# Two expert jobs of a two-layer mixture kernel: 380 and 376 slots become 384

## The chip, the cores and the metric

The kernel runs on one core of one Trainium2 chip. The metric is the device time of one execution in microseconds (us). Three runs of the kernel before took 655.56, 658.47 and 653.74 us; the median is 655.56 us.

## The reference

Attention in chunks (2 batches, 8 heads, 768 positions, head dimension 64) gives x with 1536 rows of 512 numbers. Two mixture-of-experts layers follow, with 8 experts of 512 x 1024 and 1024 x 512 weights each:

```python
# layer 1: the two best experts of every row, weighted
for e in range(E):
    for k in range(2):
        mask = top2[:, k] == e
        h = np.maximum(x[mask] @ w1[e], 0.0)
        out[mask] += top2_w[mask, k, None] * (h @ w2[e])
# layer 2: one expert of every row, up to 384 rows each, in order
logits = x @ w_gate
expert_idx = np.argmax(logits, axis=1)
...
h = np.maximum(np.einsum('ecd,edf->ecf', disp, w1), 0.0)
y = np.einsum('ecf,efd->ecd', h, w2)
out[i] = gate_w[i] * y[expert_idx[i], pos[i]]
```

How many rows an expert gets is known only on the chip, so the kernel gives every expert a fixed number of slots, and keeps loops for what does not fit.

## The kernel before, in words

**Jobs.** After the attention, TensorE works through a list of jobs; a job is an expert's slots. In layer 1, expert 0 has two jobs (`V0`, 128 slots, and `V8`, 312 slots); the other seven experts are ranked on the chip by falling count, and the expert of rank s gets job `S[s]` with `CAPS1[1 + s]` slots (line 18): 432, 412, 404, 396, 384, 380 and 376. Layer 2 begins with `U0` (256 slots), `UL` and the jobs `R`. This text is about `S[5]` (380 slots), `S[6]` (376 slots) and the beginning of layer 2.

**A job.** For each block of 128 slots, GpSimd issues a gather of 128 token rows by a list of ids (L756); this is always 128 rows, also for a last block with fewer slots. Rows are transposed by TensorE (L764). A job of at most 384 slots is of kind M. Its first layer has eight units (`layer1`): 12 products each, with the weights stationary and all slots moving (L816), so the number of slots is the number of columns. Every unit ends with `hh` on ScalarE (L827) and `hl` on VectorE (L828). Its second layer goes by blocks of 128 slots (`rows2`): the slots are stationary and 512 columns of weights move, 12 products for each half of the hidden units, 24 for a block. The block's rows are weighted on ScalarE (L878), four transposes (L886) and eight products (L893) give what they add to the second gate's logits (L894), and GpSimd issues an indirect DMA that adds them to their tokens' rows in `x2_rows` (`scatter`, L900; the profile calls both tables x_rows). The scatter takes `yr[:n]`, as many rows as the block has slots: 124 in the last block of `S[5]`, 120 in that of `S[6]`.

Idle slots point to 512 spare rows ahead of the tokens' rows, which hold zeros and are not read as tokens.

**Weights.** SyncE issues loads of half pieces (`raww`, L733); ScalarE makes the high part (`whi`, L750) and VectorE the low part (`wlo`, L751), one job ahead of their use.

**Work behind the products.** Every engine executes its instructions in the order in which the program emits them. The second layer's routing is a Python generator whose parts are emitted between products: each product adds its column count divided by 2400 to a credit (`mm3`, `tick`), and the next part is emitted when the credit reaches what the part before was estimated to cost (`COST`). So the number of columns in a job decides between which products a part stands.

One such generator is `early` (L1516 and on), started at unit 3 of `S[6]`. It loads the second gate's logits of all tokens, `lg` (`load_lg2`, L1472, on SyncE's queue). This load reads rows that the scatters of `S[5]` add to, and waits for them. Then VectorE finds every token's best expert (L399 `fm_m`, L402 and L404 `fm_e`, L407 `fm_k`, L1523 `em`), TensorE counts places from `em` (L1527, L1529), VectorE and TensorE turn them into a list of ids (L476 to L496), and two gathers fetch the first rows of `U0` (`ids_u`).

```python
# early()
load_lg2()
yield "w"
_, mk = yield from first_max(None, lg2, 128, NB1, "2", rp)
...
nc.tensor.matmul(pv, tri, e0, start=True, stop=False)   # L1527, e0 is em in the profile
```

Of the kernel before, what the change touches and what calls it, by code (L numbers as in the profile page):

```python
# [17 lines left out]
CAPS1 = [128, 432, 412, 404, 396, 384, 380, 376, 312]  # L18
# [40 lines left out]
def attention_two_moe_kernel(  # L59
# [10 lines left out]
    DM, E = w_gate1.shape  # L70
# [39 lines left out]
    # ---------------------------------------------------------------- loads  # L110
# [17 lines left out]
    def v_rows(b, i, dst, r0, h, c, dims):  # L128
        """rows of v into windows of chunks; r0: the first row's place in its window."""
        nc.sync.dma_start(dst, bass.AP(tensor=v.tensor,  # L130
                                       offset=v.offset + ((b * H + 4 * i + h) * S + 32 * c - 16 + r0) * D,
                                       ap=[[D, dims[0]], *dims[1:], [1, D]]))
# [17 lines left out]
    def v_blank(b):  # L150
        """ones for the sums; zeros where a window reaches beyond the sequence."""
        nc.gpsimd.memset(vt[b][:, :, :, D:D + 1], 1.0)
        for i in range(2):
            nc.gpsimd.memset(vt[b][64 * i:64 * i + 16, :, 0, 0:D], 0.0)
            nc.gpsimd.memset(vt[b][64 * i + 32:64 * i + 64, :, NC - 1, 0:D], 0.0)
# [7 lines left out]
    # ------------------------------------------------------------ constants  # L163
# [26 lines left out]
    # ------------------------------------------------------------ attention  # L190
# [21 lines left out]
    def t_unit(b, h, which, tag):  # L212
        """a head's keys or queries with the head's dimensions on the partitions."""
        hp, a = divmod(h, 2)
        src = raws[b, hp, which]
        pv = bank(tag)[:, 0:384].rearrange("p (r n) -> p r n", r=4)
        for r in range(4):
            nc.tensor.transpose(pv[:, r], src[:, a, 128 * r:128 * r + 128], ident[0:96, 0:96])
        o = slice(64 * a, 64 * a + 64)
        for x in range(2):  # L220
            s = pv[64 * x:64 * x + 64]
            if which == 0:
                nc.scalar.activation(
                    qz[b][o, hp, :, a].rearrange("p c (w r x) -> p x c w r", x=2, r=4)[:, x],
                    s.rearrange("p r (c w) -> p c w r", w=4), AF.Copy)
            else:
                base = kt[b][o, hp, 16 + x:17 + x]
                nc.vector.tensor_copy(
                    bass.AP(tensor=base.tensor, offset=base.offset,
                            ap=[list(base.ap[0]), [40, NC], [24, 2], [8, 2], [2, 4]]),  # L230
                    s.rearrange("p r (c u w) -> p c u w r", u=2, w=2))
                fill()

    def busy(p, n):
        """keeps the tensor engine's clock up over waits and small products; p: a bank to be written next."""
        for _ in range(n):
            nc.tensor.matmul(p, warmer[:, 0:128], warmer, start=True, stop=True)
# [4 lines left out]
    def scores(t):  # L242
        """[query of (chunk, head of a pair), (chunk pair, head pair), key of the window]"""
        b, g = divmod(t, G)
        ps = bank("A")
        pv = ps.rearrange("p (x j i k) -> p x j i k", x=2, j=2, i=2)
        for x in range(2):
            for hp in range(HP):
                for y in range(2):
                    c = 4 * g + 2 * x + y  # L250
                    nc.tensor.matmul(pv[64 * y:64 * y + 64, x, hp % 2, hp // 2],
                                     qz[b][:, hp, c].rearrange("p a n -> p (a n)"),
                                     kt[b][:, hp, 40 * c:40 * c + 64], start=True, stop=True)
        sv = ps.rearrange("p (x a k) -> p x a k", x=2, k=64)
        if g == 0:
            nc.vector.memset(sv[0:64, 0, :, 0:16], NEG)
        if g == G - 1:
            nc.vector.memset(sv[64:128, 1, :, 56:64], NEG)
        st["s", t] = ps
# [77 lines left out]
    def step(t, units):  # L337
        """probabilities and outputs of tile t, scores of tile t + 1, logits of tile t - 2."""
# [32 lines left out]
    # -------------------------------------------------------------- routing  # L371
    yid = consts.tile([128, KD, 2, 144], F32R, name="yid")
    def y_consts():
        """[identity | gate, high part | gate, low part] for the high part of y, [identity | high | 0] for the low."""
# [6 lines left out]
    def all_of(gen):  # L381
        """runs a generator to its end; what it returns."""
# [8 lines left out]
    def by_tile(pl, P, lead, T, s_, dt, name):  # L391
        """a tile of what is kept by token, for T of the tokens' tiles."""
# [3 lines left out]
    def first_max(oh, z, P, T, tag, pl):  # L396
        """oh: one-hot of the first maximum along the experts of z [P, T, E]; returns the maxima."""
# [16 lines left out]
    def places(pl, oh, pv, P, T, K, nv, tag, beyond=None):  # L414
        """of every token its slot in its expert: slot // 128, slot % 128, slot % 512."""
# [19 lines left out]
    def one_hots(pl, oh, at, tok, P, T, K, nv, nb, tag):  # L435
        """of every token the one-hot of slot % 128, and by block the token's id."""
# [35 lines left out]
    def one_list(pl, mk, pv, tok, P, T, nb, tag, mark="pp"):  # L472
        """the ids of one list's tokens (mk: whether a token is in it) by slot, less the slot."""
# [20 lines left out]
        p = bank("D")  # L494
# [4 lines left out]
    def route(i):  # L499
        """the top two experts of a batch of tiles, their weights, the tokens' ranks; the slots of the first jobs."""  # L500
# [98 lines left out]
    def enter(i):  # L599
        """a batch's tokens into the table of every expert's slots."""  # L600
# [16 lines left out]
    def ranks(cnt, nv, tag, keep=None):  # L617
        """experts (columns 0..nv of cnt) by falling count, those not to keep last: sel[s, e], and the order."""
# [27 lines left out]
    def reg_of(col, hi):  # L646
        """of a whole number on the chip a register, read when first wanted."""
# [22 lines left out]
    def out_ids(ids, raw, sh, pl, tag):  # L670
        """rows of the output; beyond its end for the idle slots."""
# [6 lines left out]
    def overflow(cnt, ce, tab, nv, nb, tag):  # L678
        """blocks with tokens beyond their expert's slots: flags, their ids, how many."""
# [35 lines left out]
    # ------------------------------------------------------------------ FFN  # L715
# [4 lines left out]
    def half(n, j, wa, wb, r, i, behind=False):  # L720
        """DMA of half a piece of an expert's weights (r: its number, in a register or not), maybe behind gathers."""
# [21 lines left out]
    def split(n, c, eng=None, at=None):  # L743
        """an operand as the sum of two float32r parts."""
# [30 lines left out]
    def tick(us):  # L775
        """work behind the products: its next parts, as the time of the products passes."""
# [26 lines left out]
    def run_until(done):  # L803
        """the work behind, as far as something needs it."""
# [41 lines left out]
    def hidden(w, c, n, between=None):  # L846
        """layer 1 by rows: a chunk of 512 of the hidden units of up to 128 slots."""
# [6 lines left out]
    def turn(c, n):  # L854
        """a chunk of the hidden units into columns, as the sum of two parts."""
# [9 lines left out]
    def rows2(n0, blk, half_, C, between=None):  # L865
        """layer 2 by rows, over half of the hidden units."""
# [14 lines left out]
    def row_columns(yr, n):  # L881
        """rows of up to 128 slots into columns."""
# [6 lines left out]
    def row_logits(yr, n):  # L889
        """what those rows add to the second gate's logits."""  # L890
# [18 lines left out]
    def y_block(g, ids_ap, blk, C, prev):  # L909
        """rows of y of up to 128 slots, weighted, with what they add to the next logits; into their tokens' rows."""  # L910
# [36 lines left out]
    class Job:  # L947
        """an expert's slots. kind: W, both layers with the weights stationary; M, the second by rows; T, both."""
# [71 lines left out]
        def rest(self):  # L1020
            """the blocks of y that are left for the next one's time."""
# [4 lines left out]
    def run_jobs(jobs, hooks, splits, raw_next):  # L1026
        """the jobs one after another; the next one's weights and rows come ahead of its products."""
# [37 lines left out]
    def picked(b_, fl, idf, nb):  # L1065
        """of the blocks that are flagged one: its expert's one-hot, its tokens' ids; the flag goes."""
# [31 lines left out]
    def rest1(wa, wb, ov, en, nb, after):  # L1098
        """the first layer's blocks of 128 tokens beyond the slots, one after another."""
# [3 lines left out]
        with tc.If(n > 0):  # L1103
            with tc.For_i(0, n):
# [9 lines left out]
                def part(src):  # L1114
                    """128 by 256 of the weights four times, each the sum of two parts."""
# [29 lines left out]
    def last_seconds(sel, n0):  # L1145
        """the last job's second block, whose weights are still there: how many, whether it has tokens; their ids."""
# [30 lines left out]
    def rest2(wa, wb, ov, en, nb):  # L1177
        """the second layer's blocks of 128 tokens beyond the slots, the last job's first."""
# [39 lines left out]
    # ------------------------------------------------------- attention, run  # L1218
    state = {"gen": [], "next": None}

    def advance():
        """a slice of the routing."""
# [35 lines left out]
    def half_step():  # L1258
        """between two parts of a step: a slice of the routing, or of the first expert's weights."""
# [130 lines left out]
    # ------------------------------------------ behind the first expert  # L1390
# [28 lines left out]
    def turns(a, b):  # L1419
        """parts of two generators in turn."""  # L1420
# [37 lines left out]
    # ----------------------------------------------------- second routing  # L1458
# [15 lines left out]
    def choose():  # L1474
        """which expert the second layer starts with: one with many of the tokens that the last job doesn't touch."""
# [40 lines left out]
    def early():  # L1516
        """the tokens of the first expert that the last job doesn't touch, and their slots."""
# [20 lines left out]
    def late():  # L1538
        """every token's expert; the slots of all, those of the first expert's early ones as they were."""
# [87 lines left out]
    def overflow_done():  # L1627
        """what is beyond the first layer's slots."""
# [106 lines left out]
```

## Time and profile before

| What | Value |
|---|---|
| Median of 3 runs | 655.56 us (653.74 to 658.47) |
| Span of the profiled execution | 655.8 us |
| PE (TensorE products) busy | 597.5 us, 91% |
| PEld (weight loads) busy | 537.0 us, 82% |
| DVE (VectorE) busy | 383.6 us, 58% |
| ACT (ScalarE) busy | 311.6 us, 48% |
| POOL (GpSimd) busy | 166.7 us, 25% |

The profiled execution's own time is known by its span, 655.8 us; the median of the runs is 0.2 us under it. All times in the rows below are counted from the start of that span. In a timeline row the number in brackets is the time that the engine stood idle before the instruction, with what ended the wait. "x4" is four instructions in a row. In a shape such as "128*124 128x512" the first pair is the stationary operand (rows x columns), the second the result's or moving size. A row with a clock gives it as a share of full speed: 1.00 is 2.4 GHz and 0.50 is 1.2 GHz.

### The profile page before, as it was taken

Reading aid. Unit: us, or ns where it says so; the run is one execution under the profiler, and the core shown is the slowest. Engines: PE = TensorE matmul, PEld = TensorE weight load, DVE = VectorE, ACT = ScalarE, POOL = GpSimd, SP = SyncE. Lnnn points to the kernel's source line nnn. Section 1 sums busy time; section 2 is a strip of 40 time slices with the busy share of each in tenths; the row PEclk is TensorE's granted clock in tenths of the full one; section 3 lists DMA queues with packets and bytes.
Section 4 is the critical chain, followed back from the end, with each engine's and each line's share of the span. In section 5 each row is a group of like instructions: output and inputs, shape, how many; then the busy total and the mean of one; then the engine's idle time right before and its main releaser. Section 6 shows DMA issues by size and latency. Waiting matters only on the chain. (4 is left out here: it accounts for less than half of the span.)

```text
span 655.8 us, 12411 instructions
## 1 busy us (share of the span) xinstructions
PE 597.5 (91%) x4569; PEld 537.0 (82%) x4569; DVE 383.6 (58%) x1007; ACT 311.6 (48%) x661; POOL 166.7 (25%) x210
## 2 busy tenths in 40 slices
PE   6477858799999999999999999979999999999994
PEld 3366747579999999999999898968978988889983
DVE  7255647678655555555555537354568647787661
ACT  4144435423554544545445545344417557686561
POOL 6040036523051221312203130302354114111110
PEclk9677967989999999999999999989999999999998
DMA  9999998517785575755636565445365577687741
GB/s 191 126 179 168 140 266 248 162 50 215 286 224 173 145 215 176 174 176 131 178 124 147 146 151 162 98 116 146 34 227 186 167 254 245 214 271 237 240 150 34
DMA packets 87939, 114.33 MB, mean 174 GB/s; under 512 B 39397, under 2 KB 39397, under 8 KB 87872
## 3 DMA queue, kind: packets, MB, share of 16 engines
q1 hardware_dynamic: 78592, 91.21, 49.4%
q0 software_dynamic: 9280, 22.26, 15.7%
q8 instruction: 38, 0.62, 0.4%
q14 instruction: 29, 0.24, 0.1%
HBM read 91.91 MB, written 22.31 MB: 174 GB/s over the span
## 5 line engine op out<-in xcount | busy, mean ns | idle before, releaser
L751 DVE TENSOR_TENSOR wlo<-raww,whi 128x512 fp32r<-128x512 f32 x232 | 159.6, 711 | 33.9 <-ACT whi L750 32.6
L750 ACT ACTIVATE whi<-raww 128x512 fp32r<-128x512 f32 x256 | 152.0, 624 | 25.6 <-DMA raww<-in_moe_w_dram 22.3
L828 DVE SCALAR_TENSOR_TENSOR hl<-psA,hh 128x256 fp32r<-128x256 f32 (+8 forms) x104 | 53.8, 518 | 80.5 <-ACT hh L827 76.1
L827 ACT ACTIVATE hh<-psA 128x256 fp32r<-128x256 f32 (+8 forms) x104 | 47.7, 458 | 109.3 <-PE psA L816 104.0
L816 PE MATMUL psA<-xh,wlo 128*128 128x256 f32 (+8 forms) x416 | 85.0, 326 | 2.6 <-DVE hl L828 1.9
L816 PE MATMUL psA<-xh,whi 128*128 128x256 f32 (+8 forms) x416 | 83.2, 321 | 0.0
L816 PE MATMUL psA<-xl,whi 128*128 128x256 f32 (+8 forms) x416 | 82.8, 321 | 0.0
L900 POOL DMA_INDIRECT x_rows<-yr,ids x25 | 39.9, 1596 | 124.8 <-ACT whi L750 81.6
L816 PEld LDWEIGHTS psA<-xh,wlo 128*128 128x128 f32 x416 | 67.1, 188 | 4.3 <-DVE hl L828 2.4
L816 PEld LDWEIGHTS psA<-xl,whi 128*128 128x128 f32 x416 | 68.6, 188 | 0.6 <-DVEq L1103 0.2
L816 PEld LDWEIGHTS psA<-xh,whi 128*128 128x128 f32 x416 | 68.7, 188 | 0.4
L756 POOL DMA_INDIRECT xg<-x_rows,ids x37 | 37.7, 1019 | 94.2 <-DVE gs L936 41.1
L816 PE MATMUL psC<-wlo,hh 128*128 128x512 f32 (+2 forms) x200 | 58.8, 414 | 0.0
L816 PE MATMUL psC<-whi,hh 128*128 128x512 f32 (+2 forms) x200 | 56.4, 400 | 0.0
L816 PE MATMUL psC<-whi,hl 128*128 128x512 f32 (+2 forms) x200 | 55.5, 399 | 0.0
L768 DVE TENSOR_TENSOR xl<-psB,xh 128x512 fp32r<-128x512 f32 (+6 forms) x36 | 23.0, 642 | 42.0 <-ACT xh L767 42.0
L751 POOL TENSOR_TENSOR wlo<-raww,whi 128x512 fp32r<-128x512 f32 x24 | 32.5, 1366 | 56.7 <-DMA x_rows<-xs 31.2
L816 PEld LDWEIGHTS psC<-whi,hl 128*128 128x128 f32 (+2 forms) x200 | 38.0, 191 | 8.8
L816 PEld LDWEIGHTS psC<-whi,hh 128*128 128x128 f32 (+2 forms) x200 | 37.9, 192 | 8.8
L816 PEld LDWEIGHTS psC<-wlo,hh 128*128 128x128 f32 (+2 forms) x200 | 36.0, 192 | 5.9
L878 ACT ACTIVATE yr<-psC,gs 128x512 f32<-128x512 f32 (+2 forms) x25 | 17.2, 687 | 47.0 <-PE psC L816 44.4
L767 ACT ACTIVATE xh<-psB 128x512 fp32r<-128x512 f32 (+6 forms) x36 | 20.0, 558 | 40.4 <-PE psB L764 38.1
(339 smaller groups left out, 924.4 us busy)
## 6 DMA issues: line engine op xcount, KB each, us to landing
raww<-in_moe_w_dram SPq DMA_DIRECT2D x128, 512.0 KB
x_rows<-zero SPq DMA_DIRECT2D x8, 520.0 KB
v<-in_v_dram SPq DMA_DIRECT2D x24, 154.0 KB
x_rows<-xs SPq DMA_DIRECT2D x12, 256.0 KB
out_dram<-zero SPq DMA_DIRECT2D x3, 1024.0 KB
raw<-in_k_dram SPq DMA_DIRECT2D x6, 384.0 KB
raw<-in_q_dram SPq DMA_DIRECT2D x6, 384.0 KB
x_rows<-zero SPq DMA_DIRECT2D x1, 1042.0 KB
```

The lines of the kernel that those rows point to most:

```text
L750: nc.scalar.activation(hi[:, c], raw, AF.Copy)
L751: (eng or nc.vector).tensor_tensor(lo[:, c], raw, hi[:, c], op=OP.subtract)
L756: return nc.gpsimd.indirect_dma_start(out=xg, out_offset=None, in_=src, in_offset=bass.IndirectOffsetOnAxis(ap=ids_ap, axis=0))
L767: nc.scalar.activation(xh[:, :, o], pv[:, :, 0:n], AF.Copy)
L768: low = lambda: nc.vector.tensor_tensor(xl[:, :, o], pv[:, :, 0:n], xh[:, :, o], op=OP.subtract)
L816: nc.tensor.matmul(ps, w[a], x[b], start=first and i == 0, stop=last and i == n - 1)
L827: nc.scalar.activation(hh[:, f, 0:C], ps[:, 0:C], AF.Relu)
L828: nc.vector.scalar_tensor_tensor(hl[:, f, 0:C], ps[:, 0:C], 0.0, hh[:, f, 0:C], op0=OP.max, op1=OP.subtract)
L878: nc.scalar.activation(yr[:n, 0:DM], ps[:n], AF.Copy, scale=g[:n])
L900: wr = nc.gpsimd.indirect_dma_start(out=x2_d, out_offset=off, in_=yr[:n], in_offset=None, compute_op=OP.add)
```

## The change

`S[5]` and `S[6]` get 384 slots each. Their layer 1 has 384 columns instead of 380 and 376; the last block of their layer 2, its rows of logits and its scatter have 128 rows instead of 124 and 120. Both remain of kind M. The gathers, the buffers' sizes (set by the largest job, 432), the number of products and of DMAs stay the same. The diff also takes out comments and the functions' doc strings, which changes no instruction.

```diff
-CAPS1 = [128, 432, 412, 404, 396, 384, 380, 376, 312]
+CAPS1 = [128, 432, 412, 404, 396, 384, 384, 384, 312]
```

The credit rises by 384/2400 for a product instead of 380/2400 or 376/2400, and so some parts of the work behind stand between other products than before. SyncE's and GpSimd's order is the same. It differs at three places, of which these two matter here.

VectorE, the last units of layer 1 of `S[6]`, before. `fm_m` to `em` are the five instructions of `early` (L399 to L1523); the first `hl` is that of unit 7 of 8, the last that of unit 8:

```order
L828 SCALAR_TENSOR_TENSOR hl<-psA,hh 128x376
L751 TENSOR_TENSOR wlo<-raww,whi 128x512
L399 TENSOR_REDUCE fm_m_5336<-lg_1763 128x12
L402 TENSOR_TENSOR fm_e_5340<-lg_1763,fm_m_5336 128x96
L404 TENSOR_TENSOR fm_e_5340<-fm_e_5340,rev 128x96
L407 TENSOR_REDUCE fm_k_5347<-fm_e_5340 128x12
L1523 SCALAR_TENSOR_TENSOR em_5351<-fm_k_5347,rev_u,fin 128x12
L828 SCALAR_TENSOR_TENSOR hl<-psA,hh 128x376
L751 TENSOR_TENSOR wlo<-raww,whi 128x512
```

The same place in the changed kernel:

```order
L399 TENSOR_REDUCE fm_m_5328<-lg_1763 128x12
L828 SCALAR_TENSOR_TENSOR hl<-psA,hh 128x384
L751 TENSOR_TENSOR wlo<-raww,whi 128x512
L402 TENSOR_TENSOR fm_e_5339<-lg_1763,fm_m_5328 128x96
L404 TENSOR_TENSOR fm_e_5339<-fm_e_5339,rev 128x96
L407 TENSOR_REDUCE fm_k_5346<-fm_e_5339 128x12
L1523 SCALAR_TENSOR_TENSOR em_5350<-fm_k_5346,rev_u,fin 128x12
L828 SCALAR_TENSOR_TENSOR hl<-psA,hh 128x384
L751 TENSOR_TENSOR wlo<-raww,whi 128x512
```

`fm_m`, which reads the loaded logits, has moved ahead of the seventh unit's `hl` and the `wlo` after it; the other four still stand behind that pair.

TensorE, the end of layer 1 of `S[6]` and the first products of its layer 2, before (L1527 and L1529 are `early`'s products, `psC` the rows of layer 2):

```order
L816 MATMUL psA<-xl,whi 128x376 x4
L816 MATMUL psA<-xh,whi 128x376 x4
L816 MATMUL psC<-wlo,hh 128x512 x2
L1527 LDWEIGHTS tri
L1527 MATMUL psD<-em_5351,tri 128x12
L1529 LDWEIGHTS ones
L1529 MATMUL psD<-em_5351,ones 128x11
```

And in the changed kernel:

```order
L816 MATMUL psA<-xl,whi 128x384 x4
L816 MATMUL psA<-xh,whi 128x384 x4
L816 MATMUL psC<-wlo,hh 128x512
L1527 LDWEIGHTS tri
L1527 MATMUL psD<-em_5350,tri 128x12
L1529 LDWEIGHTS ones
L1529 MATMUL psD<-em_5350,ones 128x11
```

The product that needs `em` stands one product of layer 2 earlier. At the third place, in layer 2 of `S[5]`, a product of the routing (L1496) also stands one product earlier.

## Rows read from the trace of the kernel before

**Rows 1.** The page: span, and the busy time of TensorE.
```profile
span 655.8 us, 12411 instructions
...
PE 597.5 (91%) x4569; PEld 537.0 (82%) x4569; DVE 383.6 (58%) x1007; ACT 311.6 (48%) x661; POOL 166.7 (25%) x210
```
**Rows 2.** Waits of PE, 140 to 656 us: total us, times, longest us.
```profile
PE psD L1527 <- DVE em L1523: 4.0, 1, 4.0
PE psA L816 <- DVE hl L828: 1.9, 2, 1.4
PE psB L764 <- DMA xg<-x_rows,ids_ul: 1.1, 1, 1.1
```
**Rows 3.** Timeline of PE, 433 to 446.2: start, us, engine, line, operation.
```profile
433.06 0.84 PE L816 MATMUL psA<-xl,whi 128*128 128x376 f32 x4
433.74 0.84 PE L816 MATMUL psA<-xh,whi 128*128 128x376 f32 x4
434.42 0.63 PE L816 MATMUL psC<-wlo,hh 128*128 128x512 f32 x2
439.05 0.17 PE L1527 MATMUL psD<-em,tri 128*128 128x12 bf16 x1 [4.01 <-DVE em L1523]
...
439.38 1.20 PE L816 MATMUL psC<-wlo,hh 128*128 128x512 f32 x2
...
443.05 1.09 PE L816 MATMUL psC<-wlo,hh 128*128 128x512 f32 x4
443.98 1.07 PE L816 MATMUL psC<-whi,hh 128*128 128x512 f32 x4
```
**Rows 4.** Timeline of DVE, 431 to 440.
```profile
433.10 0.55 DVE L828 SCALAR_TENSOR_TENSOR hl<-psA,hh 128x376 fp32r<-128x376 f32 x1 [0.83 <-ACT hh L827]
433.61 0.69 DVE L751 TENSOR_TENSOR wlo<-raww,whi 128x512 fp32r<-128x512 f32 x1
437.61 0.25 DVE L399 TENSOR_REDUCE fm_m<-lg 128x12 f32<-128x96 f32 x1 [3.31 <-DMA lg<-x_rows]
437.90 0.26 DVE L402 TENSOR_TENSOR fm_e<-lg,fm_m 128x96 f32<-128x96 f32 x1
```
**Rows 5.** Timeline of SP's queue, 424 to 450.
```profile
434.84 0.37 SPq L1472 DMA_DIRECT2D lg<-x_rows  x1
```
**Rows 6.** Timeline of POOL, 405 to 426: the second and third scatter of `S[5]`.
```profile
417.80 1.57 POOL L900 DMA_INDIRECT x_rows<-yr,ids  x1 [5.18 <-DVE yr L894]
...
423.53 2.22 POOL L900 DMA_INDIRECT x_rows<-yr,ids  x1 [4.13 <-DMA x_rows<-yr,ids]
```
**Rows 7.** DMA, 423.5 to 434.7: GpSimd's queue, packets, MB, share of the engines.
```profile
q0 software_dynamic: 512, 0.26, 17.7%
```
**Rows 8.** DMA, 417.8 to 423: busy tenths in 40 slices, then GpSimd's queue.
```profile
DMA  9996532200000000994556975799967521000000
...
q0 software_dynamic: 144, 0.27, 39.9%
```
**Rows 9.** DMA, 461.8 to 469.3: last two scatters of `S[6]`.
```profile
q0 software_dynamic: 288, 0.52, 54.4%
```
**Rows 10.** Timeline of PE, 353.5 to 357.2: layer 1 of `S[4]`, 384 columns.
```profile
353.54 0.86 PE L816 MATMUL psA<-xl,whi 128*128 128x384 f32 x4
...
356.34 0.86 PE L816 MATMUL psA<-xh,whi 128*128 128x384 f32 x4
```
**Rows 11.** Groups by form: count | busy us, mean ns.
```profile
L816 PE MATMUL psC<-whi,hl 128*128 128x512 f32 x184 | 51.2, 399 | 0.0
...
L816 PE MATMUL psC<-whi,hl 128*124 128x512 f32 x8 | 2.2, 395 | 0.0
```
**Rows 12.** Stretches: us, PE busy (instructions), granted clock, DMA share, GB/s.
```profile
439.38:445.82 6.44, 6.44 (x28) 0.79 0.26 84
```
**Rows 13.** Another stretch, same columns: layer 2 to its end.
```profile
506.00:650.00 144.00, 138.37 (x784) 1.00 0.64 211
```
**Rows 14.** Timeline of PE, 520 to 570: the longest wait in that stretch.
```profile
553.27 0.74 PE L816 MATMUL psA<-xh,wlo 128*128 128x256 f32 x4 [1.44 <-DVE hl L828]
```

## The prediction

> **What bounds the kernel now.** I read the page first: TensorE is busy for 597.5 of 655.8 us [rows 1], so the time is TensorE's work plus the moments in which it waits. Next I read what TensorE waits for from 140 us on, where the expert jobs run. The list is short, and one wait stands out: a single stop of 4.0 us at the product that needs `em` [rows 2]. The timeline of TensorE shows its place: the last four products of layer 1 of `S[6]` begin at 433.74, two products of layer 2 at 434.42, and then nothing until 439.05 [rows 3]. So this is the stage to read, and the question is what ends last there.
>
> I followed the wait back. On VectorE the `wlo` of unit 7 begins at 433.61, and then the engine stands for 3.31 us until the loaded logits are there; `fm_m` begins at 437.61, the other four follow without a gap, and 1.15 us after the start of `fm_e` (437.90) TensorE goes on [rows 3, 4]. The load of these logits was issued only at 434.84, 2.77 us before `fm_m` [rows 4, 5]. It had been waiting for the third scatter of `S[5]`, the one with 124 rows. GpSimd started that scatter at 423.53, and it took 2.22 us there instead of the 1.57 us of the second one [rows 6]. From its start to the issue of the load it is 11.3 us (434.84 - 423.53).
>
> The second scatter of the same job, with 128 rows, is quicker by far. It started at 417.80 [rows 6], and the busy tenths of its stretch of DMA go to zero after the 35th of 40 slices of 0.13 us, at 417.8 + 35 x 0.13 = 422.35: 4.6 us in all. Its packets are 144; those of the 124 rows are 512, for nearly the same bytes (0.27 and 0.26 MB) [rows 7, 8]. The last two scatters of `S[6]`, 128 and 120 rows together, are 288 packets, exactly twice 144 [rows 9]: 120 rows are not dear, 124 are.
>
> 144 is 128 rows and 16 more. 512 less 16 is 496, which is 16 x 31, and 31 is a quarter of 124. So I read the 124 rows as going over 4 of the 16 DMA engines, 31 on each, with packets of filling on the other 12, instead of 8 rows on each of 16. The Trainium skill (DMA: Bandwidth & Descriptors, section "Why a DMA increments its semaphore by 16 and not by 1") states that a DMA is spread over the largest number of engines up to 16 that divides the slowest dimension of both sides, which is 4 for 124, 15 for 120 and 16 for 128; by that rule the packet counts agree.
>
> **The change part by part.**
>
> *The scatter of `S[5]`.* With 128 rows I give it the 4.6 us of the second scatter. It starts some 0.3 us later than before (more columns ahead of it, next item): 423.8 + 4.6 = 428.4. The load of the logits can go then, and its data are usable 2.8 us later, at 431.2, where they were not before 437.61. The order gives `fm_m` its place after the `wlo` of unit 6, a unit (12 products of 0.17 us, 2.04 us) before the end of the `wlo` of unit 7, which is 434.30 [rows 4]: about 432.3 before the added columns, so there is a reserve of over 1 us, and 0.83 us more in which VectorE waits there anyway [rows 4]. The scatter may thus take almost 2 us more than I give it without changing the sum.
>
> *The columns of layer 1.* Four products of 384 columns go by in 0.70 us (353.54 to 356.34 is four times four of them) [rows 10], four of 376 in 0.68 us (433.06 to 433.74 to 434.42) [rows 3]. A job has 24 such fours in layer 1: S[6] costs 24 x 0.02 = 0.48 us more, and S[5], at half the added columns, 0.24 us. All of it is on TensorE's path: +0.72 us.
>
> *The last blocks of layer 2.* The same number of products, with 128 stationary columns instead of 124 or 120. The mean is 399 ns for 128 and 395 ns for 124 [rows 11]; 48 products at 4 ns are 0.2 us at most, and the 399 holds some products at half clock. I take zero. Transposes, weighting and logits of these blocks have the same count; they go by at the same number of instructions beside layer 1 of the next job, and I take zero for them too.
>
> *The wait for `em`.* What is late once the logits are early? Now it is the order on VectorE: `fm_e` stands behind unit 7's `hl` and `wlo`. That `wlo` ended at 434.30 [rows 4]; with 0.24 us of S[5] and 7/8 of 0.48 us of S[6] it ends at 434.96. Then 1.15 us as before, and TensorE has `em` at 436.11. TensorE itself reaches the place at 434.42 + 0.72 = 435.14, and after one product (0.23 us, a quarter of the 0.93 us between 443.05 and 443.98 [rows 3]) at 435.37. So 0.74 us of the wait are left. Before, TensorE went on at 439.05; now at 436.11, but with one product of 0.23 us more ahead of it: 439.05 - 436.11 - 0.23 = 2.71 us won, the added columns already paid.
>
> *The clock.* After the long stop TensorE's clock is granted at 0.79 on average over 439.38 to 445.82 [rows 12], which means that it spent a part of that at 1.2 instead of 2.4 GHz. The 22 products of layer 2 that stand there (24 of the first block less the two ahead of the stop) would take 22 x 0.2325 = 5.1 us at the pace of 443.05 to 443.98; they took 6.4 us. So 1.3 us go to the clock. A stop of 0.74 us should not cost that: from 506 to 650 us the clock is 1.00 [rows 13], and a stop of 1.44 us lies in that stretch [rows 14]. Bounds for this term: 0 (the clock falls all the same) and 1.3 us. I take 1.3, since 0.74 is nearer to the 1.4 that cost nothing than to the 4.0 that did.
>
> *The rest.* GpSimd is free 0.6 us earlier (2.22 to about 1.6 us), with nothing queued. On SyncE's queue the weight loads behind the load of the logits are issued earlier by what that load no longer waits; nothing waits for them before 446 us. The product at the third place (L1496) is reached at the same time as before, since 0.24 us of columns pay for 0.23 us of order. The 128-row scatter of `S[6]` has the packets that the 120 rows had.
>
> **The sum**: 2.71 + 1.3 = 4.0 us less. Against the profiled execution that is 655.8 - 4.0 = 651.8 us; the median of the runs lies 0.2 us under the span, so the forecast is **651.6 us**.
>
> **The rivals.**
>
> *Part of it is given back in layer 2 (chance 0.2).* The work behind that leads to the first rows of `U0` now has 1.3 us less of TensorE's time in which to be done, and weight loads come closer to its gathers. For this speaks that a gather of this kind already holds TensorE up by 1.1 us later on [rows 2]; against it, that the lists still follow TensorE's own products. Price: one such wait of 1.1 us up to two, 652.7 to 653.8 us.
>
> *The 124 rows are not what makes the scatter slow (0.12).* The scatter would then land as late as before for another reason, say the weight load beside it, and the change would only add columns and move the order. The logits come at 437.61 + 0.24 = 437.85; behind `fm_m` (0.29 us) now stand a `hl` (0.51) and a `wlo` (0.69) ahead of `fm_e`, then 1.15 us [rows 4]: 440.49, and one product of 0.23 us is left over. That is 440.72 - 439.05 = 1.7 us slower, 657.2 us. The price decides as soon as the logits come after 433.6 or so. Against it speak the 512 packets [rows 7], which no neighbouring scatter has. The Trainium skill names, in the same section, an exception by which software-generated direct copies on this chip are spread over all 16 engines whatever the count of partitions; by that exception 124 rows would be no worse than 128, and the change would win nothing here. This scatter is indirect, and its packets speak for the first rule.
>
> *The wait goes altogether and later waits shrink too (0.08).* The 0.74 us that I leave and the later stops of 1.1 us [rows 2] are the most that I see: 655.56 - 4.0 - 1.8 = 649.8 us.
>
> My forecast has the remaining chance, 0.6.
>
> **How the numbers follow.** The range takes in the forecast, the first rival, the third and most of the clock's bounds (652.9 us without its 1.3): 649.8 to 653.8 us. The three runs differ by 4.7 us from end to end, so a median of a few runs may lie about 1 us to either side: 648.9 to 654.8 us. Left out is the second rival and what I do not see. About 1%, or 6.6 us, is what a measurement here can tell from no change. The forecast is 0.6% faster, within it. Faster by over 1% needs under 649.0 us, the third rival or the forecast with a lucky median: 0.12. Slower by over 1% needs more than 662.1 us, which no rival gives: 0.03. Within 1%: 0.85.
>
> **What would show it.** In the profile after: the third scatter of `S[5]` has 144 packets and takes about 1.6 us on GpSimd; the load of the logits is issued at about 429 instead of 434.84; VectorE does not wait for it; TensorE's wait for `em` is 0.5 to 1 us; the granted clock in the 7 us behind it is 1.00; layer 1 of `S[6]` is 0.5 us longer. The prediction is wrong if the scatter still has 500 packets, if the clock falls behind the shorter stop, or if a new wait of TensorE of over 1 us appears between 440 and 510 us.

## The result, and the profile after

The changed kernel takes 653.04 us (median of 20 runs) against 659.88 us for the kernel before (20 runs now, the three shown ahead of the prediction among them). The ratio is **0.990**, with a 95% interval of 0.988 to 0.992: about 6.4 us less, 5.1 to 7.7. One run of the changed kernel (660.84 us) fell in a slower state of the chip; it is in the median, and the ratio and its interval leave it out.

The page of the changed kernel's profile, span and busy times, answers to [rows 1]:

```profile
span 651.2 us, 12411 instructions
...
PE 598.7 (92%) x4569; PEld 537.9 (83%) x4569; DVE 381.9 (59%) x1007; ACT 311.3 (48%) x661; POOL 165.6 (25%) x210
```

TensorE's busy time is 1.2 us longer, and the span is 4.6 us shorter. One profile of each does not settle much here: a second profile of the kernel before (E4) has 600.9 us of busy time in a span of 653.0 us. What the change does is read from the stage itself. The run that was profiled took 653.15 us, 1.95 us more than its span; the same must be allowed for the profiled execution before. The list of TensorE's waits from 140 us on (total us, times, longest us) answers to [rows 2]:

```profile
PE psB L860 <- ACT hr L852: 1.9, 1, 1.9
PE psA L816 <- DVE hl L828: 1.9, 2, 1.4
PE psB L764 <- DMA xg<-x_rows,ids_ul: 1.1, 1, 1.1
PE psD L464 <- DVE oh_L L454: 1.0, 1, 1.0
PE psD L1527 <- DVE em L1523: 0.5, 1, 0.5
```

The wait for `em` is 0.5 us instead of 4.0. A wait of 1.9 us heads the list (see E9). The timeline of TensorE at the end of layer 1 of `S[6]` answers to [rows 3]:

```profile
432.67 0.86 PE L816 MATMUL psA<-xh,whi 128*128 128x384 f32 x4
433.37 0.40 PE L816 MATMUL psC<-wlo,hh 128*128 128x512 f32 x1
434.27 0.17 PE L1527 MATMUL psD<-em,tri 128*128 128x12 bf16 x1 [0.51 <-DVE em L1523]
434.30 0.41 PE L1529 MATMUL psD<-em,ones 128*128 128x11 bf16 x11
434.57 0.94 PE L816 MATMUL psC<-wlo,hh 128*128 128x512 f32 x3
...
439.73 0.46 PE L496 MATMUL psD<-ol_R3l,ol_Ll 128*128 128x3 f16 x12
```

The stretch behind the stop has full clock (us, PE busy, granted clock, DMA share, GB/s), where [rows 12] has 0.79; it too holds 22 products of layer 2:

```profile
434.57:439.73 5.16, 5.16 (x29) 1.00 0.31 99
```

The timelines of VectorE, POOL and SP's queue, in that order, answer to [rows 4 to 6]:

```profile
430.41 0.69 DVE L751 TENSOR_TENSOR wlo<-raww,whi 128x512 fp32r<-128x512 f32 x1
431.02 0.25 DVE L399 TENSOR_REDUCE fm_m<-lg 128x12 f32<-128x96 f32 x1
431.99 0.56 DVE L828 SCALAR_TENSOR_TENSOR hl<-psA,hh 128x384 fp32r<-128x384 f32 x1 [0.73 <-ACT hh L827]
432.51 0.69 DVE L751 TENSOR_TENSOR wlo<-raww,whi 128x512 fp32r<-128x512 f32 x1
433.12 0.25 DVE L402 TENSOR_TENSOR fm_e<-lg,fm_m 128x96 f32<-128x96 f32 x1
```
```profile
421.94 1.56 POOL L900 DMA_INDIRECT x_rows<-yr,ids  x1 [4.13 <-DMA x_rows<-yr,ids]
```
```profile
426.82 0.37 SPq L1472 DMA_DIRECT2D lg<-x_rows  x1
```

The scatter takes GpSimd 1.56 us, the load of the logits is issued 4.9 us after the scatter's start instead of 11.3, and `fm_m` stands without a wait: the data are there before VectorE is. What holds `em` up now is the order on VectorE, `hl` and `wlo` of unit 7. The DMA's view from 421.9 to 427 has 144 packets on GpSimd's queue where [rows 7] has 512:

```profile
q0 software_dynamic: 144, 0.27, 42.4%
```

### The profile page after: what moved, and what is told of

The parts are those of the page before. It is cut to its first block, busy times and chain, and to the rows that moved or that the text cites. A ratio compares the mean times of both kernels' runs of the same rounds, so it can differ in the third digit from the quotient of the medians.

```text
span 651.2 us, 12411 instructions
## 1 busy us (share of the span) xinstructions
PE 598.7 (92%) x4569; PEld 537.9 (83%) x4569; DVE 381.9 (59%) x1007; ACT 311.3 (48%) x661; POOL 165.6 (25%) x210
## 5 line engine op out<-in xcount | busy, mean ns | idle before, releaser
L828 DVE SCALAR_TENSOR_TENSOR hl<-psA,hh 128x384 fp32r<-128x384 f32 (+6 forms) x104 | 53.8, 519 | 80.8 <-ACT hh L827 80.5
L827 ACT ACTIVATE hh<-psA 128x384 fp32r<-128x384 f32 (+6 forms) x104 | 47.7, 458 | 110.1 <-PE psA L816 110.1
L816 PE MATMUL psA<-xh,wlo 128*128 128x256 f32 (+6 forms) x416 | 85.2, 327 | 2.6 <-DVE hl L828 1.9
L816 PE MATMUL psA<-xh,whi 128*128 128x256 f32 (+6 forms) x416 | 83.5, 321 | 0.0
L816 PE MATMUL psA<-xl,whi 128*128 128x256 f32 (+6 forms) x416 | 83.1, 321 | 0.0
L816 PE MATMUL psC<-wlo,hh 128*128 128x512 f32 x200 | 58.3, 412 | 0.0
L816 PE MATMUL psC<-whi,hh 128*128 128x512 f32 x200 | 56.3, 400 | 0.0
L816 PE MATMUL psC<-whi,hl 128*128 128x512 f32 x200 | 55.1, 395 | 0.0
L816 PEld LDWEIGHTS psC<-whi,hh 128*128 128x128 f32 x200 | 37.9, 191 | 8.7
L816 PEld LDWEIGHTS psC<-whi,hl 128*128 128x128 f32 x200 | 37.6, 189 | 8.4
```

The lines of the kernel that those rows point to most:

```text
L816: nc.tensor.matmul(ps, w[a], x[b], start=first and i == 0, stop=last and i == n - 1)
L827: nc.scalar.activation(hh[:, f, 0:C], ps[:, 0:C], AF.Relu)
L828: nc.vector.scalar_tensor_tensor(hl[:, f, 0:C], ps[:, 0:C], 0.0, hh[:, f, 0:C], op0=OP.max, op1=OP.subtract)
```

## The experiments

Ten more runs were made: eight new kernels, and each of the two kernels once more. Ratios are to the kernel before on the same chip, with 95% intervals. The part of the trace that the change touches is measured from the first product of layer 1 of the 380-slot job to the first product of layer 2 of the model (`U0`), and split at the product that needs `em` (L1527) and at the next product of the routing (L496). These are differences of start times in the traces, in us:

| Kernel | To `em` | `em` to L496 | L496 to `U0` | Sum | Ratio |
|---|---|---|---|---|---|
| before | 61.17 | 6.77 | 15.44 | 83.38 | |
| before again (E4) | 61.14 | 7.99 | 15.44 | 84.57 | 1.001 (0.998 to 1.004) |
| after | 58.17 | 5.46 | 15.68 | 79.31 | 0.990 (0.988 to 0.992) |
| after again (E9) | 58.16 | 5.45 | 15.68 | 79.29 | 0.992 (0.989 to 0.995) |
| E1: 380 columns, block of 128 | 57.92 | 5.45 | 15.44 | 78.81 | 0.993 (0.990 to 0.996) |
| E2: 384, scatter of 124 | 62.41 | 7.37 | 15.67 | 85.45 | 1.001 (0.998 to 1.004) |
| E3: before, wait filled | 61.30 | 5.45 | 15.43 | 82.18 | 0.994 (0.990 to 0.997) |
| E5: 384, scatter of 127 | 78.77 | 7.74 | 15.68 | 102.19 | 1.022 (1.018 to 1.026) |
| E6: 384, old order | 58.48 | 5.45 | 15.50 | 79.43 | 0.990 (0.986 to 0.993) |
| E7: 376 and 376 | 57.65 | 5.45 | 15.44 | 78.54 | 0.990 (0.987 to 0.993) |
| E8: first job alone | 58.03 | 5.45 | 15.44 | 78.92 | 0.991 (0.988 to 0.994) |
| E10: 368 and 368 | 57.64 | 5.45 | 15.39 | 78.48 | 0.990 (0.987 to 0.994) |

### E1: the block without the columns

```diff
     def rows(self, blk, half_, between=None):
-        rows2(self.n0, blk, half_, self.C, between)
+        C = 384 if self is S[5] else self.C
+        rows2(self.n0, blk, half_, C, between)
...
-        n = min(128, self.C - 128 * blk)
+        n = min(128, C - 128 * blk)
```

> 380 and 376 columns and the old order on every engine; only the last block of the 380-slot job goes through layer 2 and the scatter with 128 rows (its last 4 rows are idle slots, weighted with zero). Theory A, the 124-row scatter delays the load of the logits: 144 packets, about 1.6 us on GpSimd, the load issued near 429 us, five VectorE instructions behind the wlo of unit 7 (434.3), TensorE goes on at about 435.7 instead of 439.05 with a stop of 0.8 us, and its clock stays at 1.00: 3.3 + 1.3 = 4.6 us less than before, ratio 0.993. Rival B, columns and order make the difference: as before, ratio 1.000.

GpSimd's queue in the DMA's view of 421 to 426, TensorE's product, and the stretch from it to L496:

```profile
q0 software_dynamic: 144, 0.27, 42.5%
```
```profile
433.35 0.17 PE L1528 MATMUL psD<-em,tri 128*128 128x12 bf16 x1 [0.62 <-DVE em L1524]
```
```profile
433.35:438.80 5.45, 5.45 (x35) 1.00 0.28 89
```

(One added line makes L1527 to L1528 here.) There are 144 packets, the stop is 0.62 us, the clock stays at 1.00, and the sum is 78.81: 4.6 us under the first trace of before, as theory A had it, with the old columns and the old order. So the columns and the order are not needed for the gain.

### E2: all of the change but the scatter's 4 rows

```diff
-scatter(yr, n, self.ids[blk], True, self.prev)
+scatter(yr, 124 if self is S[5] and blk == 2 else n, self.ids[blk], True, self.prev)
```

> The changed kernel (384 columns, its order, 128-row blocks), but the scatter of the first job's last block takes 124 rows as before (the 4 left out are idle slots). Theory A: 512 packets, the load issued near 435, a stop of TensorE of about 5 us and the clock at half speed behind it; by the second rival of the prediction 1.7 us slower than the kernel before, ratio 1.003. Rival B: as the changed kernel, 4 to 6 us faster than before, ratio 0.990 to 0.994.

The whole gain is gone. GpSimd's queue in the DMA's view of 421.8 to 434, and then TensorE's timeline:

```profile
q0 software_dynamic: 512, 0.26, 16.3%
```
```profile
433.12 0.40 PE L816 MATMUL psC<-wlo,hh 128*128 128x512 f32 x1
438.27 0.17 PE L1527 MATMUL psD<-em,tri 128*128 128x12 bf16 x1 [4.75 <-DVE em L1523]
```

512 packets again, and a stop of 4.75 us. Arrival at `em` is 1.24 us later than before (62.41 against 61.17): the added columns and the two VectorE instructions that now stand between `fm_m` and `fm_e`, the place of the prediction's second rival (1.7 us, of which 0.23 lie behind `em`). The ratio's interval has room for that loss and for none. With E1 this shows that the row count of one scatter, 124 or 128, decides.

### E3: the clock alone

```diff
+        busy(p, 16)
         nc.tensor.matmul(pv, tri, e0, start=True, stop=False)
```

> The kernel before, with 16 products of zeros (128 x 512, bf16, some 0.21 us each) ahead of the product that waits for em, so that TensorE works through most of the 4.0 us stop. Theory: the clock is 1.00 in the 7 us behind the stop, and the 22 products there take 5.1 instead of 6.4 us: 1.3 us less, ratio 0.998. Rival, the clock falls or the slow pace there has another cause: no gain, ratio 1.000.

`em` comes as late as before (61.30), but TensorE is busy until shortly before it, and the 5.15 us behind run at full clock (L1527 is L1528 here):

```profile
434.97 3.63 PE L237 MATMUL psD<-warmer 128*128 128x512 bf16 x16
439.21 0.17 PE L1528 MATMUL psD<-em,tri 128*128 128x12 bf16 x1 [0.61 <-DVE em L1523]
```
```profile
439.51:444.66 5.15, 5.15 (x29) 1.00 0.12 37
```

`em` to L496 is 5.45 us, as in all kernels without the long stop: the slow pace there was the clock, and the clock fell because TensorE stood. The gain, 0.6% by the ratio (0.3% to 1.0%), is larger than the 0.2% that 1.3 us would give; the next run accounts for a part of that.

### E4: the kernel before, once more

> The kernel before, once more, for a second trace of it. Between the start of layer 1 of the 380-slot job and the start of layer 2's first job the profiles of before and after differ by 4.1 us (75.6 against 71.5 us); over many runs the medians differ by 6.4 us. Theory A: the stage takes 75.6 us here too, and what the runs have beyond 4.1 us lies in stages that the change does not touch (the attention part's clock). Rival C: the stop for em or the 124-row scatter is longer in this execution, so that the stage alone makes up 6 us.

Neither theory, but something between. The stop is 3.98 us, as in the first trace, and the way to `em` is the same to 0.03 us. But TensorE's clock stays at half speed for longer. Two stretches, the second from the clock's fall, which comes 1.07 us before the end of the stop, to its rise; below, the stretch at half speed of the first trace:

```profile
435.79:443.46 7.67, 7.67 (x29) 0.65 0.35 119
434.40:441.20 6.80, 5.73 (x25) 0.50 0.32 106
```
```profile
438.80:442.20 3.40, 3.15 (x19) 0.51 0.31 121
```

The 22 products take 7.67 us here, 6.44 us in the first trace [rows 12] and 5.15 us at full clock (E3): the fall costs 2.5 us in this execution and 1.3 us in that one. By the stages, E3 is 1.2 us ahead of the first trace and 2.4 us (0.4%) ahead of this one. What decides how long the clock stays down, no run here shows. The expectation counts its 75.6 us from a later product of the same layer 1 (385.63 instead of 377.88); the difference to the changed kernel is 4.1 us by either count.

### E5: 127 rows

```diff
-scatter(yr, n, self.ids[blk], True, self.prev)
+scatter(yr, 127 if self is S[5] and blk == 2 else n, self.ids[blk], True, self.prev)
```

> The changed kernel, but the scatter of the first job's last block takes 127 rows (the one left out is an idle slot). Theory A, rows are spread over the largest number of engines up to 16 that divides their count: 127 has no divisor, so all rows go over one engine, 16 x 127 + 16 = 2048 packets, at 8.2 us for 31 rows some 33 us; the load of the logits is issued near 460 us, TensorE stops for 25 to 30 us, ratio 1.04 or more. Rival D, any count that is no multiple of 8 costs what 124 does: 512 packets, ratio 1.00. Rival E, rows are spread over 16 engines with 8 at most on each: 144 packets, as the changed kernel.

The number of packets is what theory A gave, and rivals D and E are out. The DMA's view from 423.4 to 451, then POOL, SP's queue and TensorE:

```profile
q0 software_dynamic: 2048, 0.28, 8.9%
```
```profile
423.49 4.73 POOL L900 DMA_INDIRECT x_rows<-yr,ids  x1 [4.92 <-issue]
```
```profile
450.80 0.37 SPq L1472 DMA_DIRECT2D lg<-x_rows  x1
```
```profile
455.63 0.17 PE L1527 MATMUL psD<-em,tri 128*128 128x12 bf16 x1 [21.12 <-DVE em L1523]
```

The size was off: the load goes 27.3 us after the scatter's start and not near 460, and the kernel is 2.2% slower and not 4%. I had priced a row from the 124 rows, and here a row is cheaper. What moved beside the two scatters differs. First the DMA's view of this run from 428.7 to 450.6, which has all 2048 packets and nothing of a weight load; then the second queue in the view of [rows 7], a weight load of 0.52 MB in the same time as the 124 rows:

```profile
DMA packets 2050, 0.30 MB, mean 14 GB/s; under 512 B 1921, under 2 KB 1921, under 8 KB 2048
```
```profile
q1 hardware_dynamic: 270, 0.52, 14.7%
```

127 rows take at most 21.9 us there, some 0.17 us a row. At that pace 31 rows would take 5.3 us, where the expectation goes by 8.2: a part of what 124 rows cost may be the weight load beside them, which no run here separates. The first line also shows the filling that the prediction took for granted: 1921 packets are under 512 bytes, which is all but 127 of the 2048. One row fewer than 128 makes the stage 22.9 us longer (102.19 against 79.31).

### E6: the old order

```diff
+            cols={24: 380, 28: 376}.get(n0))    # layer 1 of the two jobs: columns that the work behind counts
...
-                tick(x[b].shape[-1] / 2400)
+                tick((x[b].shape[-1] if cols is None else cols) / 2400)
```

> The changed kernel with 384 columns and 128-row blocks, but the work behind counts 380 and 376 columns as before, so that every engine has the order of the kernel before. Theory A: the order is worth little, since fm_m, which stands behind the wlo of unit 7 again, adds 0.3 us to the wait for em, and the one product ahead of it again takes 0.2 us off: stop 0.6 us, stage within 0.3 us of the changed kernel's 79.3 us, ratio 0.990 to 0.993. Rival B, the order makes the gain: the long stop is back, ratio 1.000.

Sum 79.43 against 79.31, ratio 0.990: the move of `fm_m` and of the product is worth 0.1 us once the logits are early.

### E7: 120 rows in both

```diff
-CAPS1 = [128, 432, 412, 404, 396, 384, 380, 376, 312]
+CAPS1 = [128, 432, 412, 404, 396, 384, 376, 376, 312]
```

> 376 slots for both jobs: 120 rows in both last blocks, 8 rows on each of 15 engines, and fewer columns than before. Theory A: 144 packets, the load near 428 us, stop under 1 us, clock at 1.00, and 0.24 us of columns won instead of 0.72 paid: stage 78.2 to 78.6 us, ratio 0.989 to 0.993. Rival, a full block of 128 rows is what matters: the long stop stays, ratio 1.000.

DMA's view from 422.8 to 428, and SP's queue:

```profile
q0 software_dynamic: 144, 0.25, 37.1%
```
```profile
427.85 0.37 SPq L1472 DMA_DIRECT2D lg<-x_rows  x1
```

120 rows do as well as 128. What the change does is not to fill the block; it is to leave 124.

### E8: the first job alone

```diff
-CAPS1 = [128, 432, 412, 404, 396, 384, 380, 376, 312]
+CAPS1 = [128, 432, 412, 404, 396, 384, 384, 376, 312]
```

> One part of the change alone: the first job gets 384 slots, the second keeps 376. Theory A: all of the gain sits in the first job; old order, stop 0.7 us, stage 79.0 us, ratio 0.989 to 0.993. Rival, both parts have a share: ratio nearer to 0.996.

All of the gain is in the first job: sum 78.92, 0.39 us under the whole change. In this execution a gather of layer 2 came late, and TensorE stopped for 3.64 us there; the stretch from the clock's fall on:

```profile
481.96 1.08 PE L764 MATMUL psB<-ident,xg 128*128 128x128 f32 x4 [3.64 <-DMA xg<-x_rows,ids_ul]
```
```profile
481.50:484.90 3.40, 2.94 (x9) 2.56 (x10) 1.10 (x4) 0.60 (x1) 1.04 (x2) 0.50 1.00 399
```

That gather's wait is 0.9 to 1.3 us in the other traces, so I put this stop down to that execution and not to the kernel. It is the kind of wait that the prediction's first rival named, and this version was not run again: that it is chance is not shown.

### E9: the changed kernel, once more

> The changed kernel once more, for a second trace of it. Theory A: stage 79.3 us again with a stop of 0.5 us for em and full clock behind it; the 1.9 us wait late in layer 2 that the first trace of it showed is chance and is gone, and the ratio is again 0.988 to 0.992. Rival, that wait belongs to the change and gives part of the gain back: it is there again, and the part behind the stage takes 195.8 us as in the first trace, over 1 us more than in the two traces of the kernel before (194.1 and 194.5).

The sum is the same to 0.02 us. The 1.9 us wait of the first trace is 0.3 us here, and from `U0` to the end it takes 648.56 - 454.25 = 194.3 us, against 195.8 in the first trace and 194.1 and 194.5 in the two of before. That wait does not belong to the kernel, and no loss in layer 2 is seen in this trace.

### E10: fewer slots

```diff
-CAPS1 = [128, 432, 412, 404, 396, 384, 380, 376, 312]
+CAPS1 = [128, 432, 412, 404, 396, 384, 368, 368, 312]
```

> 368 slots for both jobs (no expert of their rank has more tokens here): 112 rows in the last blocks, 7 on each of 16 engines. Theory A: 128 packets, long stop gone as in the changed kernel, and fewer columns: at 0.02 us for four products and 8 columns, 24 fours, the two jobs take 2 x 24 x 0.04 = 1.9 us less than with 384, ratio 0.986 to 0.990, the fastest version here. Rival, TensorE's own time does not count there: as the changed kernel, 0.990.

128 packets, and the long stop is gone. The sum is 0.8 us under that of the changed kernel and not 1.9. Four products of 368 columns take 0.67 us, so 0.03 and not 0.04 us are won on each four, 1.4 us in all; and a product of the routing in layer 2 of `S[5]` now waits for 0.46 us:

```profile
403.49 0.17 PE L1496 MATMUL psD<-ums,ones 128*128 128x8 bf16 x1 [0.46 <-DVE ums L1493]
```

At 0.990 (0.987 to 0.994) it cannot be told from the changed kernel, so no version here is shown to beat it.

## Why the prediction was right, and where not

**The wait and what releases it**: right. The chain scatter, load of the logits, `fm_m` to `em`, TensorE was read from the trace of before, and E1 and E2 show it from both sides: the packets of this one scatter make and unmake the stop.

**The scatter's price**: right. From its start to its last packet it took about 4.5 us (4.6 forecast; 143 of the 144 packets fall in the DMA's view of 421.94 to 426.40), and the load was issued 4.9 us after its start. The reading of the 512 packets as 16 times 31 and 16 more is borne out by E5, whose 2048 packets were forecast by the same count. The Trainium skill's rule in its page DMA: Bandwidth & Descriptors (section "Why a DMA increments its semaphore by 16 and not by 1"), the largest number of engines up to 16 that divides the rows, gave, with that count, the right packets for 112, 120, 124, 127 and 128 rows (128, 144, 512, 2048 and 144). The exception that the page makes, and makes for some direct copies only, would by my estimate give 144 for 124 and 127; the scatter here is indirect, and measured 512 and 2048.

**The wait that is left**: 0.74 us forecast, 0.51 and 0.51 measured. I had let `fm_e` start at the end of `wlo`, 0.69 us after its start; in the trace it starts 0.61 us after it (432.51 to 433.12). The other 0.16 us is how the wait is counted: I let TensorE stand from 0.23 us after the start of the one product ahead, and the profile has that product busy for 0.40 us. The cause, the order on VectorE, was as said.

**The columns and the last blocks**: right. The way to `em` shrank by 3.00 us where the terms gave 2.94 (439.05 - 436.11), and E8 against the whole change puts the second job's columns at 0.4 us (0.48 forecast).

**The clock**: the mechanism was right (E3), and this term of the sum was mis-sized. I took 1.3 us from the one trace there was; the second trace of the same kernel shows 2.5 us after the same stop, and E2 1.9 after one of 4.75 us. So the stage gains 4.1 us against the first trace and 5.3 against the second (E4 against after), while I forecast 4.0. This is a part of why the ratio, 0.990 (0.988 to 0.992), lies below my 655.8 to 651.8, 0.994. The interval's lower gains are covered by the two stages; whether the rest of its range, up to 7.7 us, is anything but spread stays open.

**The time itself**, 651.6 forecast and 653.04 measured, is near by luck in part: the three runs of before had a median 4.3 us below that of 20 runs, and the gain was taken 2.8 us too small (4.0 against 6.8 between the medians), so that the two errors cancelled but for 1.4 us. I took 655.8 us for the whole profiled execution; the profiled run of the changed kernel took 1.95 us more than its span.

**The rivals**: that a part is given back in layer 2 shows in neither trace of the changed kernel once the wait that E9 lacks is set aside; the late gather in E8 is the one sign of it, seen once. That something other than the 124 rows makes the long stop is excluded by E1 and E2; whether the weight load beside them adds to it is open (E5). The wait did not go altogether.

## What to carry to other kernels

Count the packets of an indirect DMA before a wait is blamed on contention. Here a row count whose largest divisor up to 16 is small had many packets and landed late: the load behind the scatter was issued 11.3 us after its start with 124 rows (divisor 4) and 27.3 us with 127 (divisor 1), against 4.9 us with 128; 112 and 120 rows were no worse than 128. Such a DMA costs only where something waits for it in order, here a small load that stood behind it on the way to a product. The stop of TensorE of 4 us cost more than its length, since the clock fell during it and was still at half speed behind it; one trace is not enough to price that part.

## What the runs showed of the hardware that I had not expected

- The same stop of 4.0 us put the clock at half speed for stretches of different length in two executions of one program, 3.4 and 6.8 us: 1.3 and 2.5 us lost. After the stop of 21 us in E5 the 7.5 us behind it had a granted clock of 0.68 (7.47 us for what takes 5.16 in the changed kernel). In the changed kernel's first trace the clock was 1.00 behind stops of 1.45 us (547.40 to 550.00) and 1.88 us (633.40 to 636.00).
- A row of the scatter has no fixed price here. The load of the logits, which waits for it, was issued 11.3 us after the scatter's start with 31 rows on each of 4 engines (as read from the packets), and 27.3 us after it with 127 on one.
- GpSimd's own time on a scatter follows the packets and not the rows: 1.56 us for the 144 packets of 128 rows in the changed kernel, 2.22 us for the 512 of 124 rows [rows 6], 4.73 us for the 2048 of 127 rows (E5).
